# Last output block over two PSUM banks, its stores cut and issued differently, and a new order of all steps (sigmoid attention and token-mixing MLP, one core)

## The chip, the cores and the metric

The kernel runs on one NeuronCore of a Trainium2 chip. Its engines are TensorE (PE in the profile, PEld for its weight loads), VectorE (DVE), ScalarE (ACT), GpSimd (POOL) and SyncE (SP, which only issues transfers here). The metric is the device time of one execution in microseconds; lower is better.

## The reference

```python
def _attn_ref(q, k, v):                       # 8 x 12 heads x 448 x 64
    scores = (1/sqrt(64)) * q @ k.T - log(448)
    return sigmoid(scores) @ v
def _moe_ref(x, w_q, w_k, w_out):             # x: 8 x 448 x 768, from all heads
    wq, wk = x @ w_q, x @ w_k                 # 768 -> 64
    W_tok = (1/sqrt(64)) * einsum('bsd,btd->bst', wq, wk)
    mixed = einsum('bst,btd->bsd', W_tok, x)
    return relu(mixed) @ w_out                # 768 x 768
```

All inputs and the output are float32; the kernel multiplies in bf16.

## The kernel before, in words

The 96 heads are worked in 24 groups of four ("quads", numbered n), three quads to each of the 8 batch elements u. The 448 tokens are split as 64 x 7: token = 7p + i, so a token block i has 64 rows, and two token blocks fill 128 partitions.

For a quad, q, k and v are loaded by SP into the pool `ld` of 8 float32 buffers (`load1`, L169), cast to bf16 (`cast1`, L187; mostly on POOL, some on DVE), and q and k are transposed: by PE, or by DVE's 32-block transposes, in some quads after POOL has swapped partition halves (`arrange`, L152). Then come seven score steps (letter S, `scores`, L294): four 64x64 matmuls side by side give the scores of one token block, and ACT turns 128 x 896 of them into bf16 with a sigmoid (L303). Seven value steps (P, `values`, L313) multiply by v and add up in PSUM; the result is copied to `xt`. A step x or X transposes it back (`tr_x`; X with eight whole transposes, x with 32 small ones).

After three quads of a batch element the MLP follows: W (x times w_q and w_k, `mlp_wqk`; l and L the tiled form), N (transposes), U or T (plain and tiled, `mlp_tmp`), M (mixing, with a relu that scales), and output steps O, Q, I (`out_pair`, `out_halves`, `out_chunk`), each one part of a product with w_out. A small letter, or Q for some, puts a step's copy out of PSUM on the other engine or splits it between DVE and ACT.

The order of all steps is written out by hand, or rather by a planner, in three strings: `PLAN` has one letter per step, `BANKS` the PSUM bank or pair of banks that each step takes (there are 8), and `ORDER` the order in which SP loads and POOL casts. Digits 1 and 2 in `PLAN` put a cast on DVE or ACT. Nothing reorders at run time: each engine runs its instructions in the order in which the steps issue them, and a semaphore holds an engine until what it needs is done. SP's queue is one such order: loads, copies of w_out and the stores of finished output stand in one line. A load waits for its `ld` buffer, that is for the cast eight loads before.

The change's own place is `out_chunk` (L572). A block is 128 rows (two token blocks of one batch element) by 384 columns; one part is three 128x128 matmuls with 384 columns, two parts make a block, two blocks a chunk of 128 x 768 in a tile `o`, of which three exist. The last chunk is stored in two pieces as its two halves are done, each piece as two transfers, one for each 64 rows, SP issuing one and ACT the other (L595 to L602). Its last 384 columns lie in one bank; DVE copies the first 192 of them and ACT the other 192 (L611, L612).

Of the kernel before, what the change touches and what calls it, by code (L numbers as in the profile page):

```python
# [10 lines left out]
BF16 = mybir.dt.bfloat16  # L11
# [6 lines left out]
def kernel(  # L18
# [12 lines left out]
    nc = tc.nc  # L31
    B, H, S, HD = q.shape
    D = H * HD
    DH = moe_w_q.shape[1]
    assert DH == HD == 64 and S == 448 and D == 768
    P = 128
    NI, NP = 7, 64
    NU = B
    NJ = H // 4
    NC = D // P  # L40
    NB = D // 2
    HALF = (slice(0, 64), slice(64, 128))
# [5 lines left out]
    def pool(name, bufs, **kw):  # L48
# [4 lines left out]
    p_c16 = pool("c16", 2)  # L53
    p_v16 = pool("v16", 4)
# [10 lines left out]
    banks16 = banks.rearrange("p b x -> p (b x)").bitcast(BF16).rearrange("p (b x) -> p b x", b=8)  # L65

    BANKS = (
# [11 lines left out]
    )  # L79
    BANKS = BANKS.split()[::-1]  # L80

# [12 lines left out]
    def bank1():  # L94
        b = int(BANKS.pop())
        take(b)
        return (b,), banks[:, b], banks16[:, b]

    def read(fb, inst, keep=False):

        for b in fb:
            for old in readers[b][0]:
                if not keep and old.ins.engine != inst.ins.engine:
                    tc.declare_no_dep(inst.ins, old.ins, reason="both only read the bank")
            readers[b][1].append(inst)
# [19 lines left out]
    def xt(u, j):  # L125
# [4 lines left out]


    PLAN = (
        "FFSSKFSFFSaSSbSFFSSFFSFSSrPPsPPSzPPPSSSXSqkPSPSrPPPPSPPSPPSs"
        "PPPSPzSXwSWSSWW2WWXSSNPPPSSPrPPsPSUSzSPqPSPkPSPPPSxSMSSXMSPS"
        "PcPPSSPdPPWwwSWMSWWSXrsSSOOSSOOSzPPPSPPPPSSOCONSxSUSPPSMPPcP"
        "SP1PdCSOSOSCcPPPSPxPSPPSOOSMSwdOWWSMSwOwcSSWdOOSxrSONSSOPCPP"
        "sSPPSSPPOOSPPSzPSPPPPSUPPSPxSPPPSCSCcPOwoSdMSWwOwSxSwWOSMNSO"
        "ocSMSOOdxSSOOSTPSPPSPPcPdSPPPPPSPPPSOGOSMOSQP1PSPSXPcPPSPSOO"
        "SOS1dOPSPPPGPSPPOSOxSOcSoOLdLSOSLrLsLLSOSQXSNOzSOSPOPScOSPPP"
        "PSPSUSPPP1SxPGPPRLSLldlSLScLOOSOQxSOSO1MSOQxSPPSPdPNPGPRSTOS"  # L140
        "O1SOGOSOScOxSOdSOPSPPPSP1SPPP1PPPSPPROGOGSOLcQxSlLLdSlLOSOON"
        "SOSOOSSxOQScTPdSPPPPPSPSOOSOSSOPPPPSPPROSOSxOQPSPPGPPGPpMxWW"
        "wwwwyINIIItIiIGMiIMiIIOOOOOOOQOoOQOQOQ"
    )
    KIND = ["a"] + [t for t in PLAN if t in "qacer"]

# [40 lines left out]
    def cast1(n, nm, e):  # L187
        if KIND[n] in "cer" and nm != "v":
            if n not in pq:
                pq[n] = p_c16.tile([P, 2, 2, NI, 32, 2], BF16, tag="qk16", name="qk16")  # L190
            f = pq[n]
            COPY[e](  # L192
                out=f[:, :, "qk".index(nm)].rearrange("p e i d y -> p e y i d"),
                in_=ld.pop((nm, n)).rearrange("p (y i e d) -> p e y i d", y=2, i=NI, e=2),
            )
            ld[nm + "16", n] = f
            if ("q16", n) in ld and ("k16", n) in ld:
                arrange(n, nc.gpsimd)
            return
        p = p_v16 if nm == "v" else p_c16  # L200
        t16 = p.tile([P, NI, 2, HD], BF16, tag=nm + "16", name=nm + "16")
        COPY[e](  # L202
            out=t16.rearrange("p i b d -> p b i d"),
            in_=ld.pop((nm, n)).rearrange("p b (i d) -> p b i d", i=NI),
        )
        ld[nm + "16", n] = t16
# [106 lines left out]
    def values(n, i, tail, eng):  # L313
        u, j = quads[n]
        if i == 0:
            pv[n] = bank2()
        fb, ps, _ = pv[n]
        for h in range(2):
            for g in range(2):
                nc.tensor.matmul(  # L320
                    ps[HALF[g], h, 0:S], ld["v16", n][HALF[h], i, g, :],
                    ats[n, i][HALF[h], g, :], start=(i == 0), stop=(i == NI - 1),
                )
        if i == NI - 1:
            if tail:
                for h in range(2):
                    read(fb, COPY["vs"[h]](out=xt(u, j)[:, h, 0:S], in_=ps[:, h, 0:S]))
            else:
                read(fb, COPY[eng](out=xt(u, j)[:, :, 0:S], in_=ps[:, :, 0:S]))  # L329
# [242 lines left out]
    def out_chunk(act, tail):  # L572

        if opened:
            w, m, nb, fb, ps = opened.pop()
            part = 1
        else:
            w, m, nb = chunks.pop(0)
            if nb < 0:
                nb = 0  # L580
                chunks.insert(0, (w, m, 1))
            fb, ps, _ = bank1()
            part = 0
        if nb == 0 and not part:
            ot[0] = p_o.tile([P, D], F32, tag="o", name="o")
        o = ot[0]

        def block(ps, w0, w1, c0, c1):
            for c in range(c0, c1):
                nc.tensor.matmul(  # L590
                    ps, mxs[w][:, 2 * S * c + m * P : 2 * S * c + (m + 1) * P],
                    wout16[:, c, w0:w1], start=(c == 0), stop=(c == NC - 1),
                )

        def store(cols):  # L595
            for y in range(2):
                b, i = divmod(2 * m + y, NI)
                eng = nc.scalar if tail and y else nc.sync
                eng.dma_start(
                    out=out[2 * w + b].rearrange("(p i) d -> p i d", i=NI)[:, i, cols],  # L600
                    in_=o[HALF[y], cols],
                )  # L602

        ps = ps[:, 0:NB] if not part else ps
        block(ps, nb * NB, (nb + 1) * NB, part * NC // 2, (part + 1) * NC // 2)
        if not part:
            opened.append((w, m, nb, fb, ps))
            return
        if w == NU // 2 - 1 and not chunks:
            h = NB // 2  # L610
            read(fb, nc.vector.tensor_copy(out=o[:, NB : NB + h], in_=ps[:, 0:h]), keep=True)  # L611
            read(fb, nc.scalar.copy(out=o[:, NB + h :], in_=ps[:, h:]), keep=True)  # L612
        else:
            read(fb, COPY["s" if act else "v"](out=o[:, nb * NB : (nb + 1) * NB], in_=ps), keep=True)  # L614
        split = tail and w == NU // 2 - 1 and m == NI - 1
        if nb or split:
            store(slice(nb * NB, (nb + 1) * NB) if split else slice(0, D))

    w32 = {}

# [40 lines left out]
    for t in wqks:  # L661
        nc.vector.memset(t[:, S:], 0.0)


    ORDER = (
# [4 lines left out]
    )  # L670
    BY = {"s": [], "v": []}
    for x in ORDER.split():
# [2 lines left out]
        elif x[0].isupper():  # L675
            BY["s"].append((x[0].lower(), int(x[1:])))
    OTHERS = set(BY["s"] + BY["v"])
    ORDER = [(x[0], int(x[1:])) for x in ORDER.replace(".", "").lower().split()]
    done = dict.fromkeys("SPqkKxWNUMOCgz", 0)
    used, loaded, cast = set(), set(), set()  # L680

# [2 lines left out]
    def pump_loads():  # L684
        while len(loaded) < len(ORDER):
            nm, n = ORDER[len(loaded)]
            if nm == "w" and n:
                loaded.add((nm, n))
                continue
            if len(ring) >= 8 and ring[-8] not in cast:  # L690
                break
            ring.append((nm, n))
            if nm == "w":
                load_weights()
            else:
                load1(n, nm, nc.sync)
            loaded.add((nm, n))
# [31 lines left out]
    def pump():  # L729
        while pumped[0] < len(ORDER):  # L730
            nm, n = ORDER[pumped[0]]
            if (nm, n) not in OTHERS:
                if not ready(nm, n):
                    break
                cast_now(nm, n, "g")
            pumped[0] += 1

    def cast_next(e):
# [130 lines left out]
```

## Time and profile before

| | us |
|---|---|
| median of 3 runs | 182.27 (182.17 to 184.32) |
| the profiled execution | 182.05 |
| its span, first to last instruction | 180.28 |
| PE, ACT, DVE, POOL busy | 169.6, 160.0, 142.1, 123.4 |
| granted TensorE clock | 0.996 |

The span is what the profile shows; the profiled execution's own time has 1.77 us more around it. An engine's busy time is the union of its instructions' times; PE's matmuls overlap, so PE can be shown as busy while it could take more. The page's section 5 and the groups by line give for each line of the kernel the engine, the operation, its tiles and shapes, how often it ran, its busy time and the mean of one. The chain of work that ended last is followed back from the last instruction, at each step to what released it.

### The profile page before, as it was taken

The page shows a single profiled execution, that of the slowest core. Times are in us where ns is not written, and L with a number is a line of the kernel's source. Part 1 is how long each engine was busy: PE and PEld are TensorE (multiplying, and loading weights), DVE is VectorE, ACT ScalarE, POOL GpSimd, SP SyncE. Part 2 cuts the span into 40 slices and gives each one's busy share as a digit, 9 for nine tenths or more (in the row PEclk, how much of TensorE's full clock was granted, in tenths as well). Part 3 has the DMA queues.
Part 4 walks back from the last instruction along what each step waited for, and adds up shares of the span by engine and source line. Part 5 has one row for each costly group of instructions (what it writes and reads, how often), then busy time and mean ns, then how long its engine had stood idle before and what let it go on. Part 6 is the DMA issues. An engine that isn't in the chain of part 4 may idle for free.

```text
span 180.3 us, 7970 instructions
## 1 busy us (share of the span) xinstructions
PE 169.6 (94%) x3471; PEld 112.5 (62%) x3472; DVE 142.1 (79%) x229; ACT 160.0 (89%) x212; POOL 123.4 (68%) x168
## 2 busy tenths in 40 slices
PE   7787899889999999999999999999999999999990
PEld 7333555554455445655686768778987789778560
DVE  3239599998989899889899879887999866588810
ACT  4699999999999999999999989999999899985240
POOL 1397799998998999999999999989306990000000
PEclk9999999999999999999999999999999999999998
DMA  5999999999999799989998999983946744442686
GB/s 174 356 394 387 331 382 376 288 302 364 411 340 346 181 306 292 372 285 288 313 282 285 281 374 346 316 266 96 264 118 155 226 95 107 91 91 46 157 241 175
DMA packets 24915, 47.31 MB, mean 262 GB/s; under 512 B 3888, under 2 KB 18480, under 8 KB 24880
## 3 DMA queue, kind: packets, MB, share of 16 engines
q1 hardware_dynamic: 23680, 44.84, 77.0%
q0 software_dynamic: 800, 1.18, 3.6%
q10 hardware_dynamic: 400, 0.79, 1.4%
q8 instruction: 27, 0.44, 1.0%
q14 instruction: 8, 0.07, 0.1%
HBM read 35.78 MB, written 11.01 MB: 260 GB/s over the span
## 4 chain that ended last, share of the span: by engine, by line
PE 67%; DVE 14%; DMA 9%; POOL 4%; SPq 2%; ACT 2%; issue 2%
PE banks L298 13%; PE banks L320 13%; PE banks L590 13%; PE banks L509 11%; DVE qk L232 4%; DMA k<-in_k_dram 4%; DMA v<-in_v_dram 3%; PE banks L549 3%; PE banks L395 3%; DVE xt L329 3%; POOL qk L192 3%; PE banks L358 2%; DVE qk L256 2%; DVE xn L347 1%; DMA out_dram<-o 1%
## 5 line engine op out<-in xcount | busy, mean ns | idle before, releaser
L303 ACT ACTIVATE at<-banks 128x896 bf16<-128x896 f32 x168 | 140.9, 946 | 3.6 <-PE banks L298 2.7
L298 PE MATMUL banks<-qk 64*64 64x448 bf16 x672 | 62.5, 357 | 2.5 <-DVE xt L329 1.4
L320 PE MATMUL banks<-at,v 64*64 64x448 bf16 x672 | 46.5, 350 | 0.1
L298 PEld LDWEIGHTS <-qk 64*64 64x64 bf16 x672 | 25.8, 105 | 21.1 <-issue 12.5
L509 PE MATMUL banks<-wout,mx 64*64 64x384 bf16 x672 | 36.3, 323 | 0.0
L320 PEld LDWEIGHTS <-v 64*64 64x64 bf16 x672 | 23.7, 106 | 6.9 <-issue 0.8
L509 PEld LDWEIGHTS <-mx 64*64 64x64 bf16 x672 | 23.3, 107 | 4.3
L590 PE MATMUL banks<-wout,mx 128*128 128x384 bf16 x132 | 24.8, 327 | 0.0
L192 POOL CAST qk<-q 128x896 bf16<-128x896 f32 x19 | 22.6, 1191 | 0.7 <-DMA q<-in_q_dram 0.2
L450 DVE TENSOR_SCALAR mx<-banks 128x512 bf16<-128x512 f32 (+3 forms) x24 | 21.0, 882 | 2.4 <-PE banks L477 1.6
L161 POOL COPY swap<-qk 32x448 uint32<-32x448 uint32 x28 | 15.8, 564 | 10.2 <-DVE qk L192 8.5
L192 POOL CAST qk<-k 128x896 bf16<-128x896 f32 x18 | 21.5, 1194 | 1.8 <-POOL qk L167 0.9
L329 DVE CAST xt<-banks 128x896 bf16<-128x896 f32 x19 | 20.5, 1081 | 1.4 <-PE banks L320 1.0
L202 POOL CAST v<-v 128x896 bf16<-128x896 f32 x20 | 18.4, 931 | 0.6
L590 PEld LDWEIGHTS <-mx 128*128 128x128 bf16 x132 | 11.9, 98 | 10.7 <-issue 3.9
L164 POOL COPY qk<-qk 32x448 uint32<-32x448 uint32 x28 | 16.6, 592 | 1.6
L263 DVE STREAM_TRANSPOSE qk<-qk 128x448 f32<-128x448 f32 x28 | 17.3, 630 | 0.1
L167 POOL COPY qk<-swap 32x448 uint32<-32x448 uint32 x28 | 15.8, 564 | 1.6
L232 DVE STREAM_TRANSPOSE qk<-qk 32x448 f32<-32x448 f32 x24 | 15.3, 636 | 0.6
L371 DVE COPY xn<-banks 128x1024 bf16<-128x1024 bf16 (+1 forms) x17 | 11.1, 654 | 4.6 <-PE banks L358 4.6
L614 DVE COPY o<-banks 128x384 f32<-128x384 f32 x15 | 8.2, 550 | 1.6 <-PE banks L590 0.8
L358 PEld LDWEIGHTS <-xt 64*64 64x64 bf16 x544 | 7.6, 109 | 1.9 <-issue 1.0
(87 smaller groups left out, 196.2 us busy)
## 6 DMA issues: line engine op xcount, KB each, us to landing
q<-in_q_dram SPq DMA_DIRECT2D x24, 448.0 KB, 7.0
v<-in_v_dram SPq DMA_DIRECT2D x24, 448.0 KB, 6.3
k<-in_k_dram SPq DMA_DIRECT2D x23, 448.0 KB, 7.3
out_dram<-o SPq DMA_DIRECT2D x51, 192.0 KB, 3.5
wout<-in_moe_w_out_dram POOLq DMA_DIRECT2D x2, 576.0 KB, 12.1
wout<-wout SPq DMA_DIRECT2D x12, 96.0 KB, 5.2
out_dram<-o ACTq DMA_DIRECT2D x3, 192.0 KB, 3.4
k<-in_k_dram SPq DMA_DIRECT2D x1, 256.0 KB, 5.2
```

Source lines behind the costliest of these rows:

```text
L164: eng.tensor_copy(out=w[hi, 0], in_=w[lo, 1])
L192: COPY[e](out=f[:, :, "qk".index(nm)].rearrange("p e i d y -> p e y i d"), in_=ld.pop((nm, n)).rearrange("p (y i e d) -> p e y i d", y=2, ...
L202: COPY[e](out=t16.rearrange("p i b d -> p b i d"), in_=ld.pop((nm, n)).rearrange("p b (i d) -> p b i d", i=NI),)
L232: nc.vector.transpose(out=qk[n][other : other + 32, h].rearrange("p t i n -> p (t i n)").bitcast(F32), in_=w[own : own + 32, 1 - h],)
L263: nc.vector.transpose(out=qk[n][:, t].rearrange("p t i n -> p (t i n)").bitcast(F32), in_=w)
L298: nc.tensor.matmul(sc[HALF[h], g, 0:S], qk[n][HALF[g], h, 1, i, :], qk[n][HALF[g], h, 0].rearrange("p i n -> p (i n)"), start=True, stop=True,
L303: inst = nc.scalar.activation(at, sc[:, :, 0:S], ACTF.Sigmoid, bias=attn_bias, scale=attn_scale)
L320: nc.tensor.matmul(ps[HALF[g], h, 0:S], ld["v16", n][HALF[h], i, g, :], ats[n, i][HALF[h], g, :], start=(i == 0), stop=(i == NI - 1),)
L329: read(fb, COPY[eng](out=xt(u, j)[:, :, 0:S], in_=ps[:, :, 0:S]))
L450: inst = nc.vector.tensor_scalar(dst, ps, moe_scale, 0.0, ALU.mult, ALU.max)
L509: nc.tensor.matmul(ps[HALF[x], y, 0:NB], mx[HALF[y], u, b, 64 * (i - 3 * y) : 64 * (i - 3 * y) + 64], wout16[HALF[y], slot(y, b), x * NB : ...
L590: nc.tensor.matmul(ps, mxs[w][:, 2 * S * c + m * P : 2 * S * c + (m + 1) * P], wout16[:, c, w0:w1], start=(c == 0), stop=(c == NC - 1),)
```

## The change

The last chunk's second half is now two blocks of 192 columns, each with six matmuls, in a bank each. DVE copies the first and ACT the second. The first half's 384 columns and the first 192 of the second half are stored by a new function, `store_both`: one transfer from SP for all 128 rows. The last 192 columns are stored as before in two transfers of 64 rows, one from SP, one from ACT.

```diff
+        last = w == NU // 2 - 1 and m == NI - 1
+
+        def store_both(cols):
+
+            b, i = divmod(2 * m, NI)
+            nc.sync.dma_start(
+                out=out[2 * w + b].rearrange("(p i) d -> i p d", i=NI)[i : i + 2, :, cols], in_=o[:, cols],
+            )
+
...
+        if nb and last:
+
+            if part:
+                fb, ps, _ = bank1()
+            h = NB // 2
+            c0 = NB + part * h
+            block(ps[:, 0:h], c0, c0 + h, 0, NC)
+            read(fb, COPY["vs"[part]](out=o[:, c0 : c0 + h], in_=ps[:, 0:h]), keep=True)
+            if part:
+                store(slice(c0, D))
+            else:
+                store_both(slice(c0, c0 + h))
+                opened.append((w, m, nb, fb, ps))
+            return
...
-        if w == NU // 2 - 1 and not chunks:
-            h = NB // 2
-            read(fb, nc.vector.tensor_copy(out=o[:, NB : NB + h], in_=ps[:, 0:h]), keep=True)
-            read(fb, nc.scalar.copy(out=o[:, NB + h :], in_=ps[:, h:]), keep=True)
-        else:
-            read(fb, COPY["s" if act else "v"](out=o[:, nb * NB : (nb + 1) * NB], in_=ps), keep=True)
-        split = tail and w == NU // 2 - 1 and m == NI - 1
-        if nb or split:
-            store(slice(nb * NB, (nb + 1) * NB) if split else slice(0, D))
+        read(fb, COPY["s" if act else "v"](out=o[:, nb * NB : (nb + 1) * NB], in_=ps), keep=True)
+        if last:
+            store_both(slice(0, NB))
+        elif nb:
+            store(slice(0, D))
```

The bf16 tile of v lies the other way round, so that its cast is one contiguous run, and `values` reads it accordingly. A cast by the transfer itself can be asked for by a star in `ORDER`; no entry has one, so it isn't used.

```diff
-        p = p_v16 if nm == "v" else p_c16
-        t16 = p.tile([P, NI, 2, HD], BF16, tag=nm + "16", name=nm + "16")
+        if nm == "v":
+            t16 = p_v16.tile([P, 2, NI, HD], BF16, tag="v16", name="v16")
...
-                    ps[HALF[g], h, 0:S], ld["v16", n][HALF[h], i, g, :],
+                    ps[HALF[g], h, 0:S], ld["v16", n][HALF[h], g, i, :],
```

`PLAN`, `BANKS` and `ORDER` are new throughout. The ends of `PLAN` (all that follows the last S, before and after) and the heads of `ORDER`:

```diff
-                                        PPGPPGPpMxWW
-        wwwwyINIIItIiIGMiIMiIIOOOOOOOQOoOQOQOQ
+                           PPPxPPmPPLxLlMlGLlO
+        OyOoNIItIiIMimIiMOoOOOoOoOOOOOOOQOOOO
...
-        "W2 q1 k1 k2 q2 v0 k3 q3 v1 q4 k4 v2 w0 k5 q5 w1 v3 v4 .w6 ...
+        "q1 k1 k2 q2 q3 v0 w2 k3 v1 k4 q4 v2 w0 k5 q5 w1 v3 W5 v4 ...
```

Counted over the whole plan: 168 S, 168 value steps, 85 output steps and 24 mixing steps in both. Transposing steps of the whole form X go from 7 to 10, of the small form (x, y) from 17 to 14; one plain U becomes a tiled T. Casts of v go from 20 on POOL and 4 on DVE to 22 on POOL, 1 on DVE and 1 on ACT. Quad 12 and quad 13 change places in how q and k are brought into form. After the last S stand 28 output parts before and 32 after; the four more were among the sigmoids before.

More of the change, by code (lines that the diff above doesn't have):

```diff
@@ L132 @@
     PLAN = (
[L133 to L143, printed above, removed]
+        "FFSSSFFKSSFaSbFFSrSFSFSSFSqSPPsPPSPzkPSPSPPPSxSrSsPPPPSPPSPS"
+        "PPPPSSXWzSSwWWSWWXSNSSPPPrSsPPUSPPzSPSPSPCMPPPSPSqkSSMSXSMSC"
+        "cPPPSPPxSPdPSOSwwrSSwwWWxSOSSOsOSNPPSPPzCPSPPSIISISIcPSPdPPS"
+        "PS2SPPOOSxSUSPPSMPPPcSPPSdOwWwSSMWWWoSMPPSPPPP1SSPcdOQSxSOOS"
+        "SNCSOOXcdSSOOSTSPPPSrPPCPSPPCPPSPPPSPSOwowSSSwsOzOxSwwWPSPMS"
+        "PPPPRSScSdXXOXoSMSOoNSMPPSPcPPSPPSUdSOSMOSOMoPSPPcPPSPSdPwWX"
+        "WSMSWWWXSSONOScTSOSOSOOdSPOSrOSPPPGPPSPPPSPPsPSPOSPOSOzSQSXP"
+        "cPPSPPPSPOSOdSOSxOlLlSLlLPSPPPxPP2GSPOOScOmdOSOOSNO1SQSTPPPc"
+        "S1PPSPOPSOSOQSMOSOSOdScOOSdOMSOmOP2PSPPxSPPP12SOSOSOSxOllLSl"
+        "lcSLPPPSPPPSPOOdSxSOOSOSOSONQSTPSPPPSPPPSPPPxPPmPPLxLlMlGLlO"
+        "OyOoNIItIiIMimIiMOoOOOoOoOOOOOOOQOOOO"
     )
@@ L199, in cast1 @@
             return
-        p = p_v16 if nm == "v" else p_c16
-        t16 = p.tile([P, NI, 2, HD], BF16, tag=nm + "16", name=nm + "16")
+        if nm == "v":
+            t16 = p_v16.tile([P, 2, NI, HD], BF16, tag="v16", name="v16")
+            if e == "d":
+                u, j = quads[n]
+                nc.gpsimd.dma_start(
+                    out=t16.rearrange("p b i d -> p b (i d)"),
+                    in_=v[u, 4 * j : 4 * j + 4].rearrange("(g h) (p i) d -> (h p) g (i d)", g=2, i=NI),
+                )
+            else:
+                COPY[e](
+                    out=t16.rearrange("p b i d -> p (b i d)"), in_=ld.pop((nm, n)).rearrange("p b x -> p (b x)"),
+                )
+            ld["v16", n] = t16
+            return
+        t16 = p_c16.tile([P, NI, 2, HD], BF16, tag=nm + "16", name=nm + "16")
         COPY[e](
@@ L593, in block @@
                 )
+        last = w == NU // 2 - 1 and m == NI - 1
[3 more added lines that the diff above has]
+                out=out[2 * w + b].rearrange("(p i) d -> i p d", i=NI)[i : i + 2, :, cols], in_=o[:, cols],
+            )
         def store(cols):
@@ L602, in store @@
                 )
+        if nb and last:
[7 more added lines that the diff above has]
+                store(slice(c0, D))
+            else:
+                store_both(slice(c0, c0 + h))
+                opened.append((w, m, nb, fb, ps))
+            return
         ps = ps[:, 0:NB] if not part else ps
@@ L677 @@
     OTHERS = set(BY["s"] + BY["v"])
-    ORDER = [(x[0], int(x[1:])) for x in ORDER.replace(".", "").lower().split()]
+    CASTING = {("v", int(x[2:])) for x in ORDER.split() if x[0] == "*"}
+    ORDER = [(x[0], int(x[1:])) for x in ORDER.replace(".", "").replace("*", "").lower().split()]
     done = dict.fromkeys("SPqkKxWNUMOCgz", 0)
@@ L686, in pump_loads @@
             nm, n = ORDER[len(loaded)]
-            if nm == "w" and n:
+            if nm == "w" and n or (nm, n) in CASTING:
                 loaded.add((nm, n))
@@ L734, in pump @@
                     break
-                cast_now(nm, n, "g")
+                cast_now(nm, n, "d" if (nm, n) in CASTING else "g")
             pumped[0] += 1
```

30 rows, old and new, of tables (BANKS, ORDER) are left out of this document.

## The prediction

> **What bounds the kernel now.** I read the engines' shares, then the windows by stage, then the chain of work that ended last, then the timeline of the last 12 us. Window columns: stretch, then busy us and (instructions) of PE, PEld, DVE, ACT and POOL, the granted clock, the DMA engines' mean busy share, GB/s.
>
> ```profile
> span 180.3 us, 7970 instructions
> PE 169.6 (94%) x3471; PEld 112.5 (62%) x3472; DVE 142.1 (79%) x229; ACT 160.0 (89%) x212; POOL 123.4 (68%) x168
> ```
>
> ```profile
> 10.00:20.00 10.00, 7.95 (x114) 3.54 (x117) 6.59 (x9) 9.96 (x14) 8.87 (x9) 1.00 1.09 366
> 20.00:40.00 20.00, 18.33 (x414) 11.13 (x413) 19.00 (x27) 20.00 (x26) 18.28 (x25) 1.00 1.07 343
> 40.00:60.00 20.00, 19.96 (x340) 10.26 (x332) 18.07 (x28) 19.96 (x25) 18.27 (x24) 1.00 0.97 345
> 60.00:80.00 20.00, 20.00 (x318) 10.27 (x317) 18.27 (x28) 19.51 (x25) 19.03 (x26) 1.00 0.94 301
> 80.00:100.00 20.00, 20.00 (x418) 13.49 (x419) 18.03 (x27) 19.59 (x26) 18.61 (x27) 1.00 0.92 287
> 100.00:120.00 20.00, 19.60 (x476) 14.92 (x469) 17.13 (x28) 19.36 (x27) 18.25 (x26) 1.00 0.96 328
> 120.00:140.00 20.00, 19.92 (x557) 16.47 (x553) 17.93 (x29) 19.72 (x29) 10.65 (x16) 1.00 0.60 168
> 140.00:150.00 10.00, 10.00 (x290) 8.39 (x279) 7.56 (x14) 9.19 (x12) 8.33 (x12) 1.00 0.57 150
> 150.00:160.00 10.00, 10.00 (x268) 8.01 (x261) 6.25 (x10) 9.98 (x16) 0.00 (x0) 1.00 0.43 93
> 176.00:178.00 2.00, 0.12 (x1) 0.00 (x0) 0.36 (x1) 0.32 (x1) 0.00 (x0) 1.00 0.93 264
> ```
>
> The reader is to see two engines full at once. ACT, with its 168 sigmoids, is busy to 20.00 of 20 us from 20 us on; its idle time in the eight windows from 20 to 160 us is 0 + 0.04 + 0.49 + 0.41 + 0.64 + 0.28 + 0.81 + 0.02 = 2.7 us, and that is all that a better order could win back from it. PE is full as well, and its instructions per 20 us grow from 318 to 557 toward the end: the output multiplications pile up there. The clock is 1.00, so no throttling enters.
>
> ```profile
> PE 67%; DVE 14%; DMA 9%; POOL 4%; SPq 2%; ACT 2%; issue 2%
> ```
>
> ```profile
> 168.21 7.92 PE banks L590 x48
> 176.15 0.37 DVE o L611
> 176.54 0.32 ACT o L612
> ```
>
> The chain of waits is PE for two thirds. Its end is a line of its own: 48 matmuls end at 168.21 + 7.92 = 176.13 us, DVE copies half of the last bank, ACT the other half only after it, and the stores and the end of the program take the rest, 180.28 - 176.13 = 4.15 us (the span is 180.28 to two places). The profiled execution took 182.05 us, so 1.77 us lie around the span; the median of the runs shown, 182.27, is 0.22 above it.
>
> **The change, part by part.** (a) PE's work. The 168 score, 168 value and 85 output steps stay. Three transposing steps go from 32 small transposes to 8 whole ones, one MLP step from 8 plain matmuls to 14 tiled ones, and the last six 384-column matmuls become twelve of 192.
>
> ```profile
> 18.55 0.57 PE banks L342 x8
> 86.18 0.38 PE banks L358 x32
> 52.44 0.84 PE banks L424 x8
> 88.37 0.64 PE banks L439 x14
> ```
>
> The transposes cost 3 x (0.57 - 0.38) = +0.57 us, the MLP step 0.64 - 0.84 = -0.20. For the halved matmuls: 384 columns take 7.92/48 = 165 ns, 128 columns 0.57/8 = 71 ns; on that line 192 columns take 95 ns, and 12 x 95 - 6 x 165 = +0.15 us (0 if the time goes by columns alone). Sum: +0.5 us.
>
> ```profile
> L590 PEld LDWEIGHTS <-mx 128*128 128x128 bf16 x132 | 11.9, 98 | 10.7 <-issue 3.9
> ```
>
> A rule that speaks against this edit: the Trainium skill (TensorE: Matmul & The Clock Gate, section LDWEIGHTS) gives a load of 128 columns 128/1.2 = 107 ns, whatever the matmul behind it. The row's 98 ns agrees; were the loads to set the pace, the term would be 12 x 98 - 6 x 165 = +0.19, so the sum hardly differs.
>
> (b) Work of the other engines. Durations stand behind the bar (busy us, mean ns).
>
> ```profile
> L202 POOL CAST v<-v 128x896 bf16<-128x896 f32 x20 | 18.4, 931 | 0.6
> L202 DVE CAST v<-v 128x896 bf16<-128x896 f32 x4 | 2.8, 696 | 0.0
> L329 DVE CAST xt<-banks 128x896 bf16<-128x896 f32 x19 | 20.5, 1081 | 1.4 <-PE banks L320 1.0
> L327 DVE CAST xt<-banks 128x448 bf16<-128x448 f32 x5 | 3.1, 615 | 0.5 <-PE banks L320 0.5
> L614 DVE COPY o<-banks 128x384 f32<-128x384 f32 x15 | 8.2, 550 | 1.6 <-PE banks L590 0.8 <-DMA out_dram<-o 0.7
> L448 ACT ACTIVATE mx<-banks 128x512 bf16<-128x512 f32 x7 | 4.4, 624 | 0.0
> L327 ACT CAST xt<-banks 128x448 bf16<-128x448 f32 x5 | 2.9, 589 | 0.0
> ```
>
> Casts of v go from 20 POOL, 4 DVE to 22 POOL, 1 DVE, 1 ACT. POOL gains 2 x 0.931 = 1.9 us, hidden: it is idle in whole windows from 150 us on. That the cast's target is now contiguous I cost at nothing (at best it shortens a POOL that has room). DVE loses 3 x 0.696 = 2.1 and, in copies of xt (19 to 22 whole, 5 to 2 half), gains 3 x (1.081 - 0.615) = 1.4; with three output copies less at 0.55 it ends about 2 us lighter. Between first and last sigmoid ACT has, beside them, 2 instead of 7 half relus (-5 x 0.624), 1 instead of 4 half xt copies (-3 x 0.589), and new on it two whole relus and one v cast; those three have no row; by the sigmoid of the same size, 0.946 (its row stands below), they are some 2.85: about -2 us.
>
> (c) The order. After the last score step the plan now has 32 output parts instead of 28, one value step more and one transposing step more: 4 x 7.92/16 = 2.0 us, +0.2, +0.4 = +2.6 us of PE work in the tail, taken out of the middle. If PE is the bound there, that costs nothing; if ACT is, all 2.6 are lost. PE's 20.00 beside ACT's 19.51 and a chain that is PE say nothing is lost. The lighter ACT and DVE can shrink only ACT's 2.7 us of idle; I take a third, -0.9. Bounds: -2.7 and +2.6. Moved loads (the second q of a plain quad ahead of the first v, and so on) stay in the same SP queue, at the same number; v's first cast, and the first value steps behind it, come one cast (0.93) later, under 16 buffers of sigmoids. A store that waits for its copy holds the loads behind it in SP's queue; there are as many as before, between other loads, and I cost that at nothing, inside the bounds.
>
> ```profile
> L303 ACT ACTIVATE at<-banks 128x896 bf16<-128x896 f32 x168 | 140.9, 946 | 3.6 <-PE banks L298 2.7
> v<-in_v_dram SPq DMA_DIRECT2D x24, 448.0 KB, 6.3
> ```
>
> The v cast on ACT would hold every sigmoid behind it if its load were late. The load (quad 19) may start when the buffer eight loads ahead is free, that of k of quad 17, cast before sigmoid 113; the cast stands behind sigmoid 133: 20 x 140.9/168 = 16.8 us later, against 6.3 us to land. So the last matmul ends at 176.13 + 0.5 - 0.9 = 175.7.
>
> (d) The end. Two banks take away ACT's wait for DVE: -(176.54 - 176.15) = -0.39 us. The stores: of before, the last four are 64 rows each.
>
> ```profile
> 175.38 0.48 ACT L614 COPY o<-banks 128x384 f32<-128x384 f32 x1 [0.70 <-DMA out_dram<-o]
> 176.89 0.50 ACTq L599 DMA_DIRECT2D out_dram<-o  x1
> L599 SPq DMA_DIRECT2D out_dram<-o x5: 466/468/554, 170.9 to 176.9; - x5
> out_dram<-o SPq DMA_DIRECT2D x51, 192.0 KB, 3.5
> out_dram<-o SPq DMA_DIRECT2D x2, 96.0 KB, 2.4
> ```
>
> The changed kernel stores columns 0 to 383, then 384 to 575, each by one copy whose destination counts 2 x 64 x columns, token group outermost, against 128 rows of SBUF. Every other copy of the program, before and after, counts 64 or 128 outermost on both sides. What a copy with an outer 2 costs, no row shows. One end: it spreads over all engines like the rest. Other end: it is cut along its outermost count, and 2 and 128 rows share only two equal cuts, so two of the 16 engines carry it. Then each of the two moves 98,304 + 49,152 = 147,456 bytes. An engine's rate: 366 GB/s over 16 engines that are all busy (10 to 20 us, share 1.09) is 22.9 GB/s; in the store window 264/(0.93 x 16) = 17.7. So 6.4 us, or 8.3 at the slow rate, against 0.8 when spread. I take the cut in two at 22.9 (the busy row with one queue, as here: both stores are on SP), since all copies that reach such totals have an outer count that 16 divides. The Trainium skill (DMA: Bandwidth & Descriptors, Rules for kernel authors) has it as a rule: an outermost dimension of c below 16 confines a copy to at most c engines. No run here shows it yet; by it the sum is the one below, without it the first rival's.
>
> What stands between an issue and the end of the span: 180.28 - 176.89 = 3.39 us for the last pair, of which 196,608 bytes at 366 GB/s are 0.54, so 2.85 us is fixed. The first of the two stores is issued 0.2 us before the last matmul ends (the same copy ended at 175.38 + 0.48 = 175.86 before, 0.27 ahead of it, on ACT; DVE takes 0.07 more). The second follows on SP while the first still runs, and the last pair's SP half queues behind both: +0.3. Sum: 175.7 - 0.2 + 2.85 + 6.4 + 0.3 = 185.1, + 1.77 = 186.8 us against the execution's 182.05, so **187.0** on the scale of the median.
>
> **The rivals.** (1) Not slower: the two stores spread over all engines. Then the path is SP's third issue, 0.8 us after the last matmul (three issues of 0.47 to 0.55, from -0.2 on), + 2.85 + 0.3: 175.7 + 3.9 = 179.6, or 181.6 us by the median. For it: nothing else in the trace runs below 16 engines. Against: nothing else has such a shape. It decides from three engines on: 147,456 x 2/3 bytes take 4.3 us, and the time falls to 184.9, within 2%. (2) The order wins all of ACT's idle time: 187.0 - 1.8 = 185.2, within 2%. For it: ACT and DVE are both 2 us lighter; against: PE is full in the same windows. (3) The order loses its 2.6 us as well, because the parts moved to the tail were free before: 187.0 + 0.9 + 2.6 = 190.5. For it: ACT's 20.00 from 20 to 40 us; against: the chain's 67% PE.
>
> **How the numbers follow.** Two engines with my order 0.68, since cutting along the outermost count explains every full spread that the trace has; rival 1 0.13; rival 2 0.12; rival 3 0.05; rivals 1 and 2 together (181.6 - 1.8 = 179.8 us, half of it better than 178.6) 0.02.
>
> ```profile
> GB/s 174 356 394 387 331 382 376 288 302 364 411 340 346 181 306 292 372 285 288 313 282 285 281 374 346 316 266 96 264 118 155 226 95 107 91 91 46 157 241 175
> ```
>
> The likeliest's own range takes the engine rate from 25.7 GB/s (the best slice of the page, 411 GB/s over 16: -0.7 us) to 17.7 (+1.9), and 1 us either way for the order: 185.3 to 189.5, a little inside the worst of both. For 8 in 10 it reaches down past rival 2 and stops below rival 3: 184.5 to 189.5, leaving out rivals 1, 1 with 2, and 3, 0.20 together.
>
> Faster or slower is counted from 2%, about what a measurement of this kernel can tell from no change: below 178.6 or above 185.9. Slower: 0.61 of the likeliest (its low end is inside 2%) and 0.05 = 0.66. Within 2%: 0.07 + 0.13 + 0.12 + 0.01 = 0.33. Faster: 0.01.
>
> **What would show it.** Right: after the last matmul some 9 us instead of 4.15, in which the DMA share is near 2/16 and the rate near 45 GB/s; the 192-KB store of two groups takes over 6 us to land where 192 KB took 3.5; ACT's last copy no longer behind DVE's (ACT issues five copies in the tail as before, with nothing queued behind them); the last matmul at 175 to 176.5. Wrong: a tail of 4 us with shares near 0.9 (rival 1), the last matmul before 174.5 or after 178 (rivals 2, 3), or ACT waiting for the load of v in the middle.

## The result, and the profile after

The changed kernel takes 187.94 us (median of 6 runs, 187.21 to 191.22) against 182.22 us of the kernel before on the same chip: a ratio of 1.030, 95% interval 1.023 to 1.038. Ratios here leave out executions more than 1.5% above the fastest of the same kernel. The forecast was 187.0 us, in a range of 184.5 to 189.5. The profiled execution took 188.34 us, with a span of 186.57 us; before, 182.05 and 180.28.

The last microseconds, in rows of the timeline (start, duration, engine, line, operation, count, and in brackets the idle time before it and its releaser):

```profile
167.83 8.30 PE L603 MATMUL banks<-wout,mx 128*128 128x384 bf16 x56
175.24 0.56 DVE L645 COPY o<-banks 128x384 f32<-128x384 f32 x1 [1.39 <-PE banks L603]
175.71 0.35 DVE L633 COPY o<-banks 128x192 f32<-128x192 f32 x1
175.82 1.29 SPq L613 DMA_DIRECT2D out_dram<-o  x2
176.17 0.32 ACT L633 COPY o<-banks 128x192 f32<-128x192 f32 x1 [1.49 <-PE banks L603]
176.52 0.47 ACTq L621 DMA_DIRECT2D out_dram<-o  x1
177.21 3.04 SPq L621 DMA_DIRECT2D out_dram<-o  x1
```

The first row ends at 176.13 us with the last matmul; before, it was 176.12. So in these two executions nothing of the loss lies ahead of that point, and all of it behind. ACT's last copy is released by PE and no longer by DVE, as planned: at 176.49 everything is computed and copied. Yet the span runs to 186.57, 10.44 us after the last matmul, against 4.17 before. Below, this distance is called the tail. The last row hints at where it goes: SP's issue of one small store takes 3.04 us, where such an issue took 0.47 in the row above.

The stretches of the end (busy time of PE, PEld, DVE, ACT, POOL, then the clock, DMA share and GB/s):

```profile
170.00:175.00 5.00, 5.00 (x33) 2.99 (x32) 1.67 (x3) 1.11 (x3) 0.00 (x0) 1.00 0.83 203
175.00:177.00 2.00, 1.13 (x13) 0.91 (x11) 0.82 (x2) 0.32 (x1) 0.00 (x0) 1.00 0.81 214
177.00:179.00 2.00, 0.00 (x0) 0.00 (x0) 0.00 (x0) 0.00 (x0) 0.00 (x0) 0.83 0.37 97
179.00:187.00 8.00, 0.00 (x0) 0.00 (x0) 0.00 (x0) 0.00 (x0) 0.00 (x0) 0.50 0.20 44
```

The granted clock is 1.00 until the last matmul and falls only behind it, so a slower clock isn't the cause. From 179 us on no engine computes, and the transfers move 44 GB/s where they moved 203 a few microseconds earlier. There is no shortage of bytes to move: the stores are all issued by 180.25. They are slow. The stores by their landing times (engine whose queue, count, size, median us from issue to landing):

```profile
out_dram<-o ACTq DMA_DIRECT2D x1, 192.0 KB, 3.2
out_dram<-o SPq DMA_DIRECT2D x2, 192.0 KB, 2.7
out_dram<-o SPq DMA_DIRECT2D x1, 96.0 KB
out_dram<-o ACTq DMA_DIRECT2D x1, 48.0 KB, 5.5
out_dram<-o SPq DMA_DIRECT2D x1, 48.0 KB, 8.2
```

Ordinary stores of 192 KB land in about 3 us. The two stores of the new function have no landing on record: the second row counts the one of 192 KB with an ordinary one and has the landing of the ordinary one alone, and the third row is the one of 96 KB. The trace's packet records fill the gap (a packet is one row of a block, 1,536 bytes in the 192-KB store): the last packet of the 192-KB store ends at 182.83 us, 7.0 us after its issue began at 175.82. The last two stores, a quarter of that size and of ordinary form, take 5.5 and 8.2 us. SP's stands behind the two new ones in its queue; of ACT's, the last packets run between theirs.

### The profile page after: what moved, and what is told of

Its sections match the earlier page's. It is cut to its first block, busy times and chain, and to the rows that moved or that the text cites. A ratio compares the mean times of both kernels' runs of the same rounds, so it can differ in the third digit from the quotient of the medians.

```text
span 186.6 us, 7850 instructions
## 1 busy us (share of the span) xinstructions
PE 169.3 (91%) x3412; PEld 115.2 (62%) x3412; DVE 141.6 (76%) x220; ACT 159.1 (85%) x209; POOL 125.6 (67%) x171
## 4 chain that ended last, share of the span: by engine, by line
PE 72%; ACT 15%; DMA 4%; DVE 1%; issue 1%; SPq 1%; POOL 1%
PE banks L522 15%; ACT at L316 15%; PE banks L311 15%; PE banks L333 13%; PE banks L603 12%; DMA k<-in_k_dram 4%; PE banks L562 3%; PE banks L408 3%; PE banks L371 2%; PE banks L396 2%; PE banks L355 2%; PE banks L452 2%; PE banks L476 1%; PE banks L490 1%; DVE qk L192 1%
## 5 line engine op out<-in xcount | busy, mean ns | idle before, releaser
L342 DVE CAST xt<-banks 128x896 bf16<-128x896 f32 x22 | 23.8, 1084 | 1.9 <-PE banks L333 1.5
L603 PE MATMUL banks<-wout,mx 128*128 128x384 bf16 (+1 forms) x138 | 24.3, 320 | 0.0
L192 POOL CAST qk<-k 128x896 bf16<-128x896 f32 x19 | 22.7, 1193 | 1.2 <-DMA k<-in_k_dram 0.8
L192 POOL CAST qk<-q 128x896 bf16<-128x896 f32 x18 | 21.5, 1196 | 2.7 <-DVE qk L276 1.4
L463 DVE TENSOR_SCALAR mx<-banks 128x1024 bf16<-128x1024 f32 (+3 forms) x22 | 21.3, 970 | 1.8 <-PE banks L476 0.7
L209 POOL CAST v<-v 128x896 bf16<-128x896 f32 x22 | 20.6, 952 | 1.8 <-DMA v<-in_v_dram 1.3
L164 POOL COPY qk<-qk 32x448 uint32<-32x448 uint32 x28 | 15.6, 556 | 1.6
L405 POOL COPY wq<-wqk 64x448 bf16<-64x448 bf16 x3 | 1.7, 557 | 16.0 <-DVE wqk L404 15.9
L645 DVE COPY o<-banks 128x384 f32<-128x384 f32 x12 | 6.7, 555 | 6.6 <-PE banks L603 6.3
L384 DVE COPY xn<-banks 128x1024 bf16<-128x1024 bf16 (+1 forms) x14 | 8.7, 624 | 3.1 <-PE banks L371 3.0
```

The costliest lines, as they stand in the source:

```text
L192: COPY[e](out=f[:, :, "qk".index(nm)].rearrange("p e i d y -> p e y i d"), in_=ld.pop((nm, n)).rearrange("p (y i e d) -> p e y i d", y=2, ...
L209: COPY[e](out=t16.rearrange("p b i d -> p (b i d)"), in_=ld.pop((nm, n)).rearrange("p b x -> p (b x)"),)
L463: inst = nc.vector.tensor_scalar(dst, ps, moe_scale, 0.0, ALU.mult, ALU.max)
L603: nc.tensor.matmul(ps, mxs[w][:, 2 * S * c + m * P : 2 * S * c + (m + 1) * P], wout16[:, c, w0:w1], start=(c == 0), stop=(c == NC - 1),)
```

## The experiments

The theory to test: a store whose destination counts two groups outermost is carried by two DMA engines, and that alone makes the loss; the new order gains a little. The rivals: the merged shape, or the single queue, is slow for another reason; or the order of steps takes part in the loss. Runs 1 to 4, 5 to 8 and 9 to 12 each shared one chip with the kernel before, whose medians there were 182.87, 182.53 and 183.15 us. Each run's ratio is to the kernel before on its chip; in brackets its 95% interval. Diffs are against the changed kernel where nothing else is said.

**1. All of the change, but four stores of 64 rows instead of two of 128.** All four come from SP.

```diff
-            nc.sync.dma_start(
-                out=out[2 * w + b].rearrange("(p i) d -> i p d", i=NI)[i : i + 2, :, cols], in_=o[:, cols],
-            )
+            for y in range(2):
+                nc.sync.dma_start(
+                    out=out[2 * w + b].rearrange("(p i) d -> p i d", i=NI)[:, i + y, cols], in_=o[HALF[y], cols],
+                )
```

> Undoes the shape of two stores alone: each 2 x 64-row store of the changed kernel becomes two 64-row stores, all four from SP; order, banks and copies stay. Two engines (my theory): the last matmul at 176.1, then 2.85 + 0.3 us behind SP's fifth issue, about 1.8 us after it, less than that if the last pair is small: 181.5 to 182.5 us. Rival, the new order or the halved matmuls cost the time: 187 to 188.5 as before this edit. Rival, SP's queue is too slow with three stores in it: five stores in it make it 188 or more.

Measured: 182.95 us, 1.0005 [0.9965, 1.0045], tail 5.33; the time is a little above the expected range. The same bytes, from the same queue, in twice as many stores, and the loss is gone: it is the form of the two copies. What the tail has beyond the 4.17 us of the kernel before fits SP's line. Its end:

```profile
174.88 2.39 SPq L614 DMA_DIRECT2D out_dram<-o  x4
175.23 0.32 ACT L634 COPY o<-banks 128x192 f32<-128x192 f32 x1 [1.49 <-PE banks L603]
177.37 0.55 SPq L622 DMA_DIRECT2D out_dram<-o  x1
```

Four issues take 2.39 us, so the fifth, ready at 175.55 when ACT's copy ends, starts at 177.37.

**2. The order alone.** New `PLAN`, `BANKS` and `ORDER` and the new layout of v, with the end of the kernel before:

```diff
-        "45 67 23 0 1 4 5 6 7 2 3 0 1 4 "
+        "45 67 23 0 1 4 5 6 7 2 3 0 1 "
...
-        if nb and last:
...
-        if last:
-            store_both(slice(0, NB))
-        elif nb:
-            store(slice(0, D))
+        if w == NU // 2 - 1 and not chunks:
+            h = NB // 2
+            read(fb, nc.vector.tensor_copy(out=o[:, NB : NB + h], in_=ps[:, 0:h]), keep=True)
+            read(fb, nc.scalar.copy(out=o[:, NB + h :], in_=ps[:, h:]), keep=True)
...
```

> The new order of all steps with the old end (one bank for the last 384 columns, four 64-row stores, two from SP and two from ACT). Two engines: the order moved the last matmul not at all (176.13 in both profiles), so 182.0, between 181.5 and 182.6. Rival, the order costs the time: 186 to 188.

Measured: 181.38 us, 0.9914 [0.9871, 0.9958], tail 4.17: the tail of the kernel before. The time is just below the expected range, which had no gain from the order. It was timed again on the third chip:

> The new order with the old end once more, beside the two above on one chip: ratio 0.990 to 0.993, as it was.

There it took 182.32 us, 0.9941 [0.9900, 0.9981], a touch less gain than expected. Both intervals exclude no gain: the order is worth 0.6 to 0.9%, 1.1 to 1.6 us. The end of the first of these runs:

```profile
175.17 0.36 DVE L624 COPY o<-banks 128x192 f32<-128x192 f32 x1 [0.36 <-PE banks L603]
175.56 0.32 ACT L625 COPY o<-banks 128x192 f32<-128x192 f32 x1 [1.86 <-DVE o L624]
175.91 0.50 ACTq L612 DMA_DIRECT2D out_dram<-o  x1
```

Here ACT does wait for DVE, and still its last store is issued 0.78 us after the last matmul (175.13), against run 1's SP store at 2.17 us (last matmul 175.20). That difference of 1.39 us can account for run 1's 1.16 us of longer tail, and so for the order's gain that run 1 lacks.

**3. The end alone.** The order of the kernel before, one bank more in `BANKS`, and the changed kernel's end, with the layout of v as before; against the kernel before:

```diff
-        "45 01 67 45 01 2 3 4 5 6 7 0 1 "
+        "45 01 67 45 01 2 3 4 5 6 7 0 1 2 "
...
+            else:
+                store_both(slice(c0, c0 + h))
...
+        if last:
+            store_both(slice(0, NB))
```

> The old order with the new end: two banks and the two 2 x 64-row stores. Two engines: all of the loss, 187.0 to 188.5. Rival, the order costs the time: 181.5 to 182.5.

Measured: 189.30 us, 1.0315 [1.0242, 1.0389], tail 10.61; the time is 0.8 us above the expected range. The end makes the whole loss under either order. That the changed kernel should be better than this one by the order's 0.6 to 0.9% the medians can't show: 1.0303 and, timed again, 1.0315, each to 0.7% either way.

> The changed kernel itself once more on the same chip, for the difference to the new order with the old end: 6 to 7 us above it, ratio 1.028 to 1.034.

The changed kernel's second timing gave 189.49 us, 1.0315 [1.0247, 1.0382], tail 10.54. That is 7.2 us above run 11 on the same chip, where 6 to 7 were expected.

**4. One store of the new form instead of two.** Columns 384 to 575 go as two stores of 64 rows from SP (`store_pair`, with run 1's body), the first 384 columns as in the changed kernel.

```diff
-                store_both(slice(c0, c0 + h))
+                store_pair(slice(c0, c0 + h))
```

> The changed kernel with the second 2 x 64-row store (192 columns) made two 64-row stores; the first (384 columns) stays. Two engines: 98,304 bytes on each of the two engines instead of 147,456, so 2.1 to 2.5 us less than the changed kernel: 185.2 to 186.0, since an engine's time goes by its bytes. Rival, a fixed price of the shape per store: half the loss, 185.0. Rival, SP's queue: one store more than in the changed kernel, 188.

Measured: 186.92 us, 1.0199 [1.0124, 1.0273], tail 8.70. That is 1.74 us of tail less than the changed kernel, where the bytes taken off the two engines (49,152 each at 22.9 GB/s) made 2.15. Direction and most of the size hold; the gain was overestimated and the time came out above what was expected. The rival, a fixed price for each store of the new form, would have taken half the loss away; the tail lost 1.74 of 6.27 us, nearer to the third of the bytes that went.

**5 and 6. The number of engines without the merged form.** Run 1's stores, with 62 of the 64 rows in each and then with 60 (the diff is against run 1). The last rows of columns 0 to 575 of the last chunk are not stored: two of each 64, then four. Up to the 16 engines, 62 rows can be cut evenly into 2 parts at most, 60 rows into 15.

```diff
-                    out=out[2 * w + b].rearrange("(p i) d -> p i d", i=NI)[:, i + y, cols], in_=o[HALF[y], cols],
+                    out=out[2 * w + b].rearrange("(p i) d -> p i d", i=NI)[0:62, i + y, cols],
+                    in_=o[64 * y : 64 * y + 62, cols],
```

> The four-store version (each 2 x 64-row store as two stores from SP) with 62 of the 64 rows in each of these four: the last two rows of each token block of columns 0 to 575 of the last chunk are not stored. Two engines, because 62 rows cut evenly only into 2 (up to 16): each of two engines carries 2 x 31 rows of 1536 and 2 x 31 of 768 bytes, 142,848 bytes, so about the changed kernel's time, 186.5 to 189. Rival, what is slow is one copy over both token groups (its shape, or its 128 rows): no such copy is left, 182.5 to 183.5.

> The same with 60 rows instead of 62 (four rows of each token block not stored). Two engines: 60 rows cut into 15, so nothing is slow: 182.5 to 183.5, the four-store version's time. Rival, any row count other than 64 or 128 is slow: 186 to 189.

Measured: with 62 rows 188.78 us, 1.0302 [1.0219, 1.0384], tail 10.22; with 60 rows 182.81 us, 1.0038 [0.9994, 1.0083], tail 4.85. The end by stretches, 62 rows first (last matmul at 177.24):

```profile
177.00:179.00 2.00, 0.24 (x3) 0.01 (x1) 0.16 (x1) 0.32 (x1) 0.00 (x0) 1.00 0.87 185
179.00:181.00 2.00, 0.00 (x0) 0.00 (x0) 0.00 (x0) 0.00 (x0) 0.00 (x0) 0.57 0.35 56
181.00:185.00 4.00, 0.00 (x0) 0.00 (x0) 0.00 (x0) 0.00 (x0) 0.00 (x0) 0.50 0.23 59
```

With 60 rows (last matmul at 174.92):

```profile
177.00:179.00 2.00, 0.00 (x0) 0.00 (x0) 0.00 (x0) 0.00 (x0) 0.00 (x0) 1.00 0.34 97
179.00:181.00 2.00, 0.00 (x0) 0.00 (x0) 0.00 (x0) 0.00 (x0) 0.00 (x0) 0.75 0.00 0
```

Two rows in 64 more or less decide 5.4 us of tail. With 62 rows 56 to 59 GB/s on the mean trickle for 6 us; with 60 rows nothing is left to move 4.1 us after the last matmul. So neither the merged form nor the 128 rows are needed for the loss: what counts is into how many equal pieces the outermost counts of both sides can be cut. The Trainium skill (DMA: Bandwidth & Descriptors, section on why a DMA increments its semaphore by 16) states it as the largest number up to 16 that divides both outermost sizes; that gives 2 for 62 rows, 15 for 60, and 2 for 2 against 128. The changed kernel and these two runs agree with it.

The packet records show the two engines themselves. In the changed kernel, from 179.9 to 180.5 us, where no other store has a packet in flight, the 1,536-byte packets run in two chains. In each a packet starts every 61 ns and takes 65, so that 2.1 are in flight on the mean. With 62 rows the mean is 2.1 as well (181 to 182 us). With 60 rows up to 13 of these packets are in flight at once. In run 1 up to 17 are, and all 128 of them are through in 0.88 us, against 5.32 in the changed kernel.

**7. Two queues.** The first of the two stores from ACT, the second from SP; `store_both` is now given the engine.

```diff
-            store_both(slice(0, NB))
+            store_both(slice(0, NB), nc.scalar)
```

> The changed kernel with the first 2 x 64-row store issued from ACT and the second from SP. Two engines: the same 147,456 bytes on the same two engines, from two queues: 186.5 to 189, as before. Rival, the bound is one queue's order (SP takes its packets one after the other): the two run side by side and the smaller one is hidden, 184 to 185.5.

Measured: 188.79 us, 1.0348 [1.0286, 1.0410], tail 10.82. The last two stores' landings:

```profile
out_dram<-o SPq DMA_DIRECT2D x1, 48.0 KB, 8.5
out_dram<-o ACTq DMA_DIRECT2D x1, 48.0 KB, 7.6
```

In the changed kernel the ACT one took 5.5 us; now both are held up. While packets of both queues' copies were in flight, the row was:

```profile
181.00:185.00 4.00, 0.00 (x0) 0.00 (x0) 0.00 (x0) 0.00 (x0) 0.00 (x0) 0.56 0.13 45
```

A share of 0.13 is two engines in 16, and 45 GB/s is the two engines' rate, for both queues together. By the packet records 1.1 packets of ACT's copy and 1.0 of SP's were in flight on the mean (181.0 to 184.3 us), so the two copies share the same two engines. A second queue wins nothing, so SP's line isn't the bound.

**8. The same form where other work could hide it.** Run 2, with five stores in the first pair of batch elements as single copies over both groups; the rest as in run 2 (the diff is against run 2).

```diff
+            b, i = divmod(2 * m, NI)
+            if w == 0 and i + 1 < NI:
+                nc.sync.dma_start(
+                    out=out[2 * w + b].rearrange("(p i) d -> i p d", i=NI)[i : i + 2, :, cols], in_=o[:, cols],
+                )
+                return
```

> The new order with the old end; five chunk stores of the first two batch elements (between 45 and 90 us) go as one 2 x 64-row copy of 768 columns each instead of two 64-row stores. Two engines: 196,608 bytes on each of two engines, 8.6 us apiece; the loads behind them in SP's queue need the same two engines and land up to 8 us later than 6 to 8 us: slower, by 2 to 15 us, as POOL and DVE wait for loads. Rival, only the end of the program feels a slow copy: 181.4, as the new order with the old end.

Measured: 199.26 us, 1.0921 [1.0855, 1.0988], 16.7 us above the kernel before, where 2 to 15 were expected. The waits of this kernel (total, times, longest) show how it gets onto the path:

```profile
POOL qk L192 <- DMA k<-in_k_dram: 11.2, 5, 6.2
...
DVE o L535 <- DMA out_dram<-o: 8.2, 1, 8.2
PE banks L311 <- DVE o L535: 7.8, 1, 7.8
```

DVE waits 8.2 us for a tile `o` that a slow store still reads, PE waits for DVE's bank, and POOL for loads of k that share SP's queue with the stores. The stretch that suffers most, here:

```profile
80.00:100.00 20.00, 16.11 (x276) 9.53 (x275) 14.41 (x21) 16.49 (x22) 17.31 (x26) 1.00 0.68 215
100.00:120.00 20.00, 15.47 (x286) 11.84 (x286) 10.84 (x16) 13.05 (x16) 13.08 (x16) 0.91 0.62 201
```

and in run 2, from which this run differs by the five stores alone:

```profile
80.00:100.00 20.00, 20.00 (x367) 12.96 (x365) 18.59 (x26) 19.44 (x27) 18.69 (x26) 1.00 0.89 300
100.00:120.00 20.00, 20.00 (x476) 15.14 (x477) 17.75 (x27) 19.56 (x26) 18.02 (x24) 1.00 0.96 323
```

PE falls from 20.00 us in both to 16.11 and 15.47, ACT from 19.44 and 19.56 to 16.49 and 13.05. Against run 2 the five stores cost some 18 us by the two ratios, 3.6 us each, where the expectation took 8.6 us for each copy alone. So the middle of the kernel hides a part of a slow store, but far from all.

**9 and 10. The best of both?** The new order and the two banks, with all stores of 64 rows: the first half's two from SP and ACT (run 9) or SP and GpSimd (run 10), the second half's two from SP and ACT after both copies. `store_pair` is now given the two engines. Run 9:

```diff
-                store_both(slice(c0, c0 + h))
...
-                store(slice(c0, D))
+                store_pair(slice(NB, D), (nc.sync, nc.scalar))
...
-            store_both(slice(0, NB))
+            store_pair(slice(0, NB), (nc.sync, nc.scalar))
```

> The new order and the two banks, with 64-row stores only: the first half from SP and ACT as soon as it is copied, the second half (both banks, 384 columns) from SP and ACT as soon as both copies are done. Two engines: nothing is slow any more, and ACT's last copy need not wait for DVE's, only for its own store issue (0.50 us): 0.2 us better than the new order with the old end, ratio to before 0.988 to 0.992. Rival, the halved matmuls or the second bank cost something: 0.993 or more.

> The same with the first half's second store issued from POOL instead of ACT, so that ACT's last copy waits for nothing but its matmuls: 0.4 us better than the new order with the old end if POOL's store lands in time, ratio 0.987 to 0.991. Rival, a store issued from POOL lands later than all others (its loads of w_out took 12 us for 576 KB): 0.995 or more.

Measured: 182.64 us, 0.9949 [0.9906, 0.9992], and 183.10 us, 0.9967 [0.9924, 1.0010]; tails 4.36 and 4.53. The gain that the two banks should add isn't there: run 11, the order alone on the same chip, took 182.32 us, and both ratios lie where the rivals had them. In run 10 GpSimd's store isn't what came last: it was issued at 177.77 us and landed after 3.2, ACT's was issued at 178.20 and also landed after 3.2. Run 9's end (last matmul at 176.30):

```profile
175.99 0.50 ACTq L613 DMA_DIRECT2D out_dram<-o  x1
176.61 0.32 ACT L633 COPY o<-banks 128x192 f32<-128x192 f32 x1 [1.76 <-PE banks L603]
176.96 0.50 ACTq L613 DMA_DIRECT2D out_dram<-o  x1
```

ACT copies without waiting for DVE, and its store is issued 0.66 us after the last matmul instead of run 2's 0.78; but the tail is 0.19 longer. By the packet records, from the last packet to the end of the span it took 1.48 us in run 9 and 1.26 in run 2, so the gain is lost there; why is open. No version measured faster than the order alone.

## Why the prediction was right, and where it was off

**The cut in two** carried the forecast, and it was right. Runs 1 and 3 show that the loss is the two copies, runs 5 and 6 and the packet records that it is the number of engines and not the shape. Rival 1 (spread over all engines) is refuted by the tail of 10.4 to 10.6 us.

**Its size** was the term most wrong: a tail of 10.44 us instead of 9.35. The first of the two copies was issued 0.31 us before the last matmul ended (forecast 0.2). From there to the end of the span it took 10.75 us, against the forecast's 2.85 + 6.4 + 0.3 = 9.55. The trace's packet records divide it: 1.69 us to the first packet of a new-form store (177.51), 7.57 us of data (to 185.08), 1.49 us to the end of the span. So the fixed part was 3.18 instead of 2.85 and the data part 7.57 instead of 6.7. The engine's rate itself was well taken: a packet of 1,536 bytes took 65 ns and one of 768 bytes 36 ns, 64 of each per engine make 6.5 us. Of the other 1.1 us, eight long packets of the first store, 104 to 386 ns each and all before 179.1 us, make 0.8 per engine on the mean. Two of these ran while no other store's packet was in flight, so why they are long is open. The two engines also didn't finish together. The signs that the prediction named, 45 GB/s and a share near 2/16, have to be read where nothing else is in flight: from 179 us on the rate is 44 and the share 0.20, but that stretch mixes the last pair's packets with an idle end. These two stretches hold the two engines, and then one of them, alone:

```profile
182.90:184.40 1.50, 0.00 (x0) 0.00 (x0) 0.00 (x0) 0.00 (x0) 0.00 (x0) 0.50 0.14 46
184.50:185.00 0.50, 0.00 (x0) 0.00 (x0) 0.00 (x0) 0.00 (x0) 0.00 (x0) 0.50 0.07 23
```

Both signs are met there, and 23 GB/s for one engine agrees with the forecast's 22.9.

**The order** was forecast at -0.9 us, with 0.5 for more PE work against it. Net of both it measured -1.6 and -1.1 us (runs 2 and 11), more gain than the net forecast of about -0.5 and inside the bounds. Rival 3 (the order loses 2.6) is refuted, and rival 2 (it wins all of ACT's idle time, 2.7 us) isn't reached. Where the gain comes from stays open: the last matmul of one and the same kernel ended at 175.13 in run 2 and at 176.83 in run 11, so one profile can't place a gain of 1 us. The changed kernel's single profile, 176.13, seemed to say that the order gave nothing; its ratios say otherwise.

**The end's details**: the prediction gave ACT's freed wait -0.39 us, but its sum runs over SP's stores and doesn't contain it. The wait did go, in every kernel with two banks, but runs 9 and 10 show no shorter tail, so that gain was wrong. In the changed kernel it couldn't matter, since SP's stores end last. ACT and DVE were forecast about 2 us lighter each; over the whole span ACT fell from 160.0 to 159.1 us and DVE from 142.1 to 141.6.

**The small terms.** The six halved products more cost nothing that shows. The stretch of output products at the end, with them in run 1 and without them in run 2:

```profile
165.26 9.94 PE L603 MATMUL banks<-wout,mx 128*128 128x384 bf16 x66
165.20 9.93 PE L603 MATMUL banks<-wout,mx 128*128 128x384 bf16 x60
```

That is 0.01 us, where the prediction had +0.15, with 0 if the time goes by columns alone and +0.19 if the weight loads set the pace. The casts of v on POOL and the one on ACT (mean ns, then the idle time before them):

```profile
L209 POOL CAST v<-v 128x896 bf16<-128x896 f32 x22 | 20.6, 952 | 1.8 <-DMA v<-in_v_dram 1.3
L209 ACT CAST v<-v 128x896 bf16<-128x896 f32 x1 | 0.9, 930 | 0.0
```

On POOL a cast takes 952 ns, against 931 before: no faster for the contiguous layout. ACT didn't wait before its cast, so that sign of a wrong forecast didn't appear.

The total came out 0.9 us above the forecast: +1.1 from the tail and +0.4 from a later last matmul (176.13 instead of 175.7), less 0.6, since the profiled execution was 0.4 slower than the median and not 0.2 faster. So that the errors partly cancel is luck; the mechanism isn't.

## What to carry to other kernels

Before joining two transfers into one, look at the outermost count on both sides: in these runs the largest number up to 16 that divides both fits the DMA engines that work for it, and 62 rows against 60, or two groups against 64 rows in each of two stores, was worth about 5 us at the end of a 182-us kernel. The Trainium skill (DMA: Bandwidth & Descriptors, Rules for kernel authors) advises one transfer over 128 partitions instead of two over the halves; here the pairs took 1.0005 times the kernel before (run 1) and the single copies 1.030, so that advice needs the check of its other rule, on the outermost size, first. Where an order of steps and an end are changed together, time each alone: here a gain of 0.6 to 0.9% was buried under a loss of 3%.

## What was unexpected of the hardware

A store in the way of a slow one is held up too, whatever its own form: 48 KB in 64 rows landed after 8.2 us behind the two copies, and in run 6, with copies of 90 and 45 KB ahead of it, such stores took 1.9 to 2.7.

```profile
out_dram<-o SPq DMA_DIRECT2D x2, 90.0 KB, 2.6
out_dram<-o SPq DMA_DIRECT2D x2, 45.0 KB, 2.3
out_dram<-o ACTq DMA_DIRECT2D x1, 48.0 KB, 2.7
out_dram<-o SPq DMA_DIRECT2D x1, 48.0 KB, 1.9
```

And the issue itself can stall: SP's last store took 3.04 us to issue, and 3.13 in the second profile, against 0.55 and 0.48 for the same store in runs 1 and 6. It doesn't always: with the same two slow stores ahead of it, it took 0.92 us in run 3, and 1.46 behind run 5's four. Run 3's tail is as long (10.61), so the stall doesn't make the tail. What decides how long an issue stalls isn't shown. In run 8, where loads stand behind the slow stores in SP's queue, one of the five slow stores took 4.12 us to issue.
